# A Performer attention and MLP-Mixer kernel on one core: batch 1's keys loaded ahead of the first half of w_ch1, with an order of the work found anew

## The chip, the core and the metric

The kernel runs on one core of one Trainium2 chip. The core has TensorE (PE, with its weight loads PEld), VectorE (DVE), ScalarE (ACT), GpSimd (POOL) and SyncE (SP), and DMA engines that all of them feed. The metric is the device time in microseconds of one execution; the median over seven runs before the change is 288.76.

## What is computed

Eight batches, eight heads, 576 positions, head size 64, 128 random features; then a mixer of 512 channels with 256 token features and 1536 channel features.

```python
def phi(x):
    proj = np.einsum('bhsd,md->bhsm', x, omega)
    sq = np.sum(x * x, axis=-1, keepdims=True) / 2.0
    h = proj - sq
    h = h - np.max(h, axis=-1, keepdims=True)
    return np.exp(h) / np.sqrt(m)
q_p, k_p = (phi(q_s), phi(k_s))          # q_s, k_s: q and k times 1/sqrt(sqrt(D))
kv = np.einsum('bhsm,bhsd->bhmd', k_p, v)
z = np.sum(k_p, axis=2)
num = np.einsum('bhsm,bhmd->bhsd', q_p, kv)
den = np.einsum('bhsm,bhm->bhs', q_p, z)[..., None] + 1e-06
x = num / den                             # heads side by side: (8, 576, 512)
...
h = np.maximum(xt @ w_tok1, 0.0) @ w_tok2 # xt: x with positions and channels swapped
u = x + h.transpose(0, 2, 1)
h2 = np.maximum(u @ w_ch1, 0.0) @ w_ch2
return u + h2
```

## The kernel before

**Stages.** For each batch `attention` makes the features of keys (L638) and queries (L652) as matmuls with the transposed omega, takes exponentials on ACT (L514), the maximum over the features of each key and its reciprocal on DVE (L664, L666), scales v by it on POOL (L671, tile `vs`), sums keys times v on PE (L684, then a copy, L701), and forms numerator and denominator on PE (L720, L722), which DVE divides (L729, L730) or, for two heads of batch 0, ACT (L742). The last 64 positions of every head (the "tail") are packed together: L546 and L558 or L514 (`kpt`) for keys, L611 (`qpt`) for queries, and the tile `vbd`, which POOL makes (L562, L565, L596), holds their v. `token_mix` (batch 0: `token_mix_first`, L803 to L825) follows with w_tok1 and w_tok2; `channel_mix` multiplies by w_ch1 (L854; for the first two blocks of batch 0 L860 and L862), applies the relu (L874, L876), multiplies by w_ch2 (L892) and stores through SP. `token_tail` (L835) does the token mixing of two batches' tails together. From batch 1 on the attention of a batch is interleaved on PE with the channel mixing of the batch before.

**Loads.** Keys of batch 0 are loaded in four pieces from ACT's and SP's queues (`load_first`, L397). Everything else that is cast to 16 bits goes through POOL's queue: q, v and tails of batch 0 (L313, L331, L324, L345), w_tok1 (L432, L436), w_tok2 (L438), the halves of w_ch1 (`load_wc1`, L444), batch 1's keys (`load_nat(1, "k", 0, 8, ...)`, again L313), their tail and v's tail, the second half of w_ch1, batch 1's queries and v, and the two halves of w_ch2 (L459). Queries and keys of batches 0 and 1 are transposed on PE (L485, tails L505). Those of later batches are cast into DRAM (L353, L358, L364) and come back transposed through SP (L374).

**What sets the order.** Every piece of work is a `Job` with an engine, a planned cost, a key and dependencies. `Planner.run` walks through a planned time: of the jobs of an engine that can start first, the one with the lowest key is taken, and it calls the function that issues the instructions. So each engine's instruction order is fixed when the program is built. A DMA job has also a planned length `wire`; all planned transfers run one after the other, a transfer's data is taken to be there `AFTER` behind its end, and PE is planned to start `MARGIN` (or a smaller value for a transfer) behind what it needs. `LANES` is 8: a queue's DMA is planned to wait for the one eight before it. A DMA on POOL comes after the one that stands before it in the code (`job.after`), whatever the keys say. The keys are tables of numbers: `HEAD` for batch 0 and the loads of the head, `NEAR` for batches 1 and 2, `KEYS` for the rest. Until the first channel mixing, the planner fills planned idle time of PE with matmuls of zeros into free banks (L943), which keep PE busy and compute nothing of the result.

Of the kernel before, what the change touches and what calls it, by code (L numbers as in the profile page):

```python
# [13 lines left out]
AX = mybir.AxisListType  # L14


KEYS = {"a": -1.349, "as": 0.099, "t": -1.509, "ts": 0.187, "gv": 2.165, "lt": -2.428, "lv": -3.989, "to": -2.341, "tt": 0.635, "ks": 1.094, "km": 0.303, "vs": -0.113, "l1": -0.452, "kt": -0.062}
NEAR = {"1": {"a": -1.734, "as": 0.259, "t": -2.775, "ts": 0.45, "gv": -0.056, "km": -2.03, "vs": -0.397, "kt": 0.253}, "2": {"a": -2.686, "as": 0.0, "t": -0.603, "ts": 0.324, "gv": -1.313, "km": 3.931, "vs": 0.571, "lv": -3.347, "lt": -2.872, "kt": -0.122}}
HEAD = {"kp": [-3.838, -3.822, -3.881, -3.404], "ke": [-2.728, -2.927, -2.827, -2.727], "km": [-4.039, -3.592, -4.221, -2.25], "vs": [-3.448, -3.487, -3.196, -2.472], "qp": [-3.203, -3.403, -3.303, -3.488], "qe": [-3.328, -3.374, -2.153, -3.748], "kv": [-3.407, -3.257, -2.676, -3.133], "ko": [-2.32, -3.035, -3.463, -3.168], "n": [-3.199, -3.47, -3.182, -2.377, -2.999, -3.268, -2.999, -2.899], "no": [-4.124, -3.487, -3.919, -3.144, -3.226, -3.426, -3.126, -2.386], "ktm": -3.643, "kt": -4.584, "kte": -5.022, "qt": -3.759, "qte": -5.587, "kx": [-6.213, -5.658, -5.326, -5.458], "kxo": [-6.855, -7.05, -5.723, -4.783], "ktx": -5.661, "ktxo": -5.912, "qx": [-4.987, -3.488], "qxo": [-4.073, -2.977], "qtx": -4.584, "qtxo": -3.371, "t1": [0.229, -1.008, -0.737, -0.359], "re": [0.072, -0.781, 0.181, -0.024], "ut": [0.056, -0.48, -0.104, -0.341], "uo": [-0.099, -0.259, -0.108, 0.38], "vbd": -8.41, "w1": -9.7, "w1t": -9.38, "w2t": -9.78, "wa": -8.03, "wb": -9.17, "w2": -10.08}
BY = {"kx": "ADDD", "ktx": "A", "qx": "DD", "qtx": "A", "ko": "DADD", "re": "AAAA", "uo": "AADD", "no": "DDADDADD", "r0": "AAAAADAAADAA", "ko1": "DDAA", "r1": "AAAAAAAAAAAA"}  # L20


# [15 lines left out]
class Planner:  # L38
# [5 lines left out]
    MARGIN = {"PE": 0.3, "ACT": 0.05, "DVE": 0.05, "POOL": 0.05, "SP": 0.0}  # L44
    LANES = 8
    BEFORE = {"POOL": 1.5, "SP": 0.8, "ACT": 0.8}
    AFTER = 0.8
    SWITCH = 0.1
    COLD = 5.5

# [25 lines left out]
    def run(self):  # L76
# [6 lines left out]
        while any(waiting.values()):  # L83
            choice = None
            for eng, jobs in waiting.items():
                ready = []
                for j in jobs:
                    t = at[eng]
                    ok = True
                    if j.after is not None and j.after.end is None:  # L90
                        continue
                    for d in j.deps:
                        if d.end is None:
                            ok = False
                            break
                        m = self.MARGIN[eng] if d.eng != eng else (-self.LATENCY["PE"] if eng == "PE" else 0.0)
                        if eng == "PE" and self.warm is not None:
                            m = min(m, 0.05)
                        if eng == "PE" and d.wire:
                            m = 0.5  # L100
                        t = max(t, d.end + m)
                    if not ok:
                        continue
                    self.now = t
                    got = []
                    for tag, name in j.take:
                        if (tag, name) in self.held:
                            continue
                        one = self.find(tag, got)
                        if one is None:  # L110
                            ok = False
                            break
                        got.append((tag, one[0]))
                        t = max(t, one[1])
                    if not ok:
                        continue
                    if j.wire and len(lanes[eng]) >= self.LANES:
                        t = max(t, lanes[eng][-self.LANES])
                    key = j.key - (KEYS["ks"] if eng == "PE" and j.rows and last_rows == j.rows else 0.0)
                    ready.append((t, key, j))  # L120
                if not ready:
                    continue
                first = min(r[0] for r in ready)
                t, _, j = min((r for r in ready if r[0] <= first + 1e-6), key=lambda r: r[1])
                if choice is None or t < choice[0]:
                    choice = (t, j)
# [3 lines left out]
            t, j = choice  # L130
            eng = j.eng
            waiting[eng].remove(j)
            if self.warm is not None and eng == "PE":
                if j.heavy:
                    self.warm = None
                else:
# [9 lines left out]
                    t = max(t, at["PE"])  # L146
# [31 lines left out]
def kernel(  # L178
# [12 lines left out]
    nc = tc.nc  # L191
# [129 lines left out]
    def load_nat_tail(b, w, key, deps=()):  # L321
        o = 0 if w == "q" else ST
        def go():
            nc.gpsimd.dma_start(  # L324
                out=nat["t", b][o : o + ST].rearrange("p i e -> p (i e)"), in_=src[w][b, :, SM:S, :].rearrange("h (g f) d -> h g (f d)", g=8)
            )
        ld[w + "t", b] = dma("POOL", key, 0.4, go, deps, cost=0.6)

    def load_v(b, key, deps=(), h0=0, h1=H):
        def main():  # L330
# [5 lines left out]
    def load_v_tail(b, key, deps=()):  # L336
        jobs = []
        for g in range(2):
            def tails(g=g):
                if b < NPE:  # L340
                    o, i = t_vt[place("vt", b)][:, g, :], v[b, 4 * g : 4 * g + 4, SM:S, :].rearrange("h (r e) d -> h r (e d)", e=2)
                else:
                    o = t_vt[place("vt", b)][g * ST : (g + 1) * ST].rearrange("p a (c d) -> p (a c) d", c=2)
                    i = v[b, :, SM:S, :].rearrange("(a i) t d -> i t a d", i=2)[g]
                nc.gpsimd.dma_start(out=o, in_=i)  # L345
            jobs.append(dma("POOL", key + 0.01 * g, 0.22 if b < NPE else 0.4, tails, take=[("vt", b)], deps=deps, cost=0.7))
        ld["vt", b] = jobs[-1]

    def load_transposed(b, key, deps=()):
# [45 lines left out]
    def load_first(h0, h1, eng, key):  # L395
        def go():
            (nc.sync if eng == "SP" else nc.scalar).dma_start(  # L397
                out=first_k[:, h0:h1, :], in_=k[0, h0:h1, 0:SM, :].rearrange("h (p j) d -> p h (j d)", j=NJ))
        job = dma(eng, key, 0.37 * (h1 - h0), go, cost=0.47)
        for h in range(h0, h1):  # L400
            ld["k", 0, h] = job

# [32 lines left out]
    def load_w1t(o, key):  # L435
        j_w1t.append(dma("POOL", key, 0.2, cost=0.58, fn=lambda: nc.gpsimd.dma_start(out=w1t[o * ST : (o + 1) * ST, o, :], in_=moe_w_tok1[SM:S, :]), deps=[j_w1tz]))  # L436
    load_w1t(0, HEAD["w1t"])
    j_w2 = dma("POOL", HEAD["w2"], 1.7, lambda: nc.gpsimd.dma_start(out=w2, in_=moe_w_tok2.rearrange("(i p) s -> p i s", p=P)))  # L438
    def w2_of(tb, j):
        return w2[:, tb, 0:SM].rearrange("p (c j) -> p j c", j=NJ)[:, j, :]  # L440
    j_wc1 = []
    def load_wc1(i):
        c0 = i * (DC // 2)
        j_wc1.append(dma("POOL", HEAD[("wa", "wb")[i]], (3.9, 4.4)[i], lambda: nc.gpsimd.dma_start(  # L444
            out=wc1[:, :, c0 : c0 + DC // 2], in_=moe_w_ch1[:, c0 : c0 + DC // 2].rearrange("(i p) c -> p i c", p=P))))
    load_wc1(0)
    load_nat(1, "k", 0, 8, -9.61)
    load_nat_tail(1, "k", -3.48)
    load_v_tail(1, -3.46)
    load_wc1(1)  # L450
# [525 lines left out]
```

The softmax here doesn't subtract the row's maximum and nothing guards it: scores larger than these inputs give would overflow.

## Time and profile before

| | us |
|---|---|
| median of 7 runs | 288.76 |
| lowest, highest | 288.64, 289.54 |
| profiled execution | 288.68 |
| its span in the profile | 286.8 |
| batch 0's channel mixing starts (first L860) | 26.43 |
| batch 0's product with w_ch2 starts (first L892) | 43.90 |
| first and last PE instruction | 1.20, 282.7 |

The profile is of one execution; times in it count from the start of its span. A line of the order of time gives start, length, engine, source line, operation, what is written and read, and in brackets the idle time of the engine before it with what ended it. Runs of equal instructions are merged, so a length is that of the whole run, with the pipeline's end in it: eight matmuls of 512 columns show 1.9 us, while the next one starts 1.73 us after the first. Landings of single DMAs are read from the trace's semaphore events.

### The profile page before, as it was taken

How to read it: one execution, taken by the hardware profiler on the slowest of the kernel's cores; microseconds unless marked ns; L12 is line 12 of the kernel's file. 1: busy time of each engine (PE TensorE's matmuls, PEld its weight loads, DVE VectorE, ACT ScalarE, POOL GpSimd, SP SyncE). 2: the span in 40 equal slices, each digit the busy share in tenths (PEclk: the TensorE clock that was granted, in tenths of full speed). 3: DMA queues.
4: the chain of work that ended last, by engine and by line, in shares of the span. 5: the costliest groups of instructions: out<-in, count | busy, mean ns of one | idle time of the engine just before them, and what ended most of it. 6: DMA issues, size and time to landing. Idle time of an engine off the chain costs nothing.

```text
span 286.8 us, 5605 instructions
## 1 busy us (share of the span) xinstructions
PE 279.7 (98%) x2186; PEld 140.7 (49%) x2186; DVE 152.3 (53%) x330; ACT 153.8 (54%) x322; POOL 93.8 (33%) x126
## 2 busy tenths in 40 slices
PE   7999999999999999999999999999999999999994
PEld 3576454445544544455445544554455444444442
DVE  4886854546669624845584647564686231031012
ACT  3995872098449552875386528753576402602600
POOL 8995940157015701480148016601141000000000
PEclk9999999999999999999999999999999999999999
DMA  8999999999966995999799988996621042013013
GB/s 191 191 201 194 202 213 152 210 228 155 166 97 161 140 173 114 214 152 185 111 197 157 201 112 146 199 199 82 129 74 39 0 110 112 0 49 115 2 45 101
DMA packets 85721, 39.59 MB, mean 138 GB/s; under 512 B 64384, under 2 KB 80128, under 8 KB 85504
## 3 DMA queue, kind: packets, MB, share of 16 engines
q0 software_dynamic: 34288, 17.45, 44.1%
q1 hardware_dynamic: 50624, 21.01, 33.5%
q10 hardware_dynamic: 784, 0.79, 0.8%
q8 instruction: 17, 0.28, 0.4%
q14 instruction: 8, 0.07, 0.1%
HBM read 35.88 MB, written 16.52 MB: 183 GB/s over the span
## 4 chain that ended last, share of the span: by engine, by line
PE 94%; ACT 2%; DMA 2%; issue 0%; SPq 0%; DVE 0%; DVEq 0%; ACTq 0%
PE bank L892 33%; PE bank L854 32%; PE bank L776 4%; PE bank L759 4%; PE bank L684 3%; PE bank L720 3%; PE bank L652 3%; PE bank L638 3%; DMA wc<-in_k_dram 2%; PE bank L760 1%; ACT kp L514 1%; PE bank L485 1%; PE bank L835 1%; PE bank L722 1%; PE bank L803 1%; PE bank L819 1%
## 5 line engine op out<-in xcount | busy, mean ns | idle before, releaser
L892 PE MATMUL bank<-wc,r 128*128 128x512 f16 (+2 forms) x444 | 100.7, 374 | 0.0
L874 ACT ACTIVATE r<-bank 128x512 f16<-128x512 f32 x106 | 62.7, 606 | 64.5 <-PE bank L854 64.4
L854 PE MATMUL bank<-uT,wc 128*128 128x512 f16 x376 | 88.7, 379 | 0.0
L892 PEld LDWEIGHTS <-r 128*128 128x128 f16 x444 | 40.9, 98 | 48.9 <-issue 4.4
L854 PEld LDWEIGHTS <-wc 128*128 128x128 f16 x424 | 39.7, 98 | 43.0 <-issue 0.4
L514 ACT ACTIVATE qp<-bank 128x512 f16<-128x512 f32 x64 | 35.6, 640 | 13.0 <-PE bank L652 13.0
L664 DVE TENSOR_REDUCE km<-kp 128x8 f16<-128x1024 f16 x32 | 38.5, 1202 | 2.3 <-ACT kp L514 2.3
L514 ACT ACTIVATE kp<-bank 128x512 f16<-128x512 f32 x64 | 34.6, 626 | 6.6 <-PE bank L638 6.4
L901 DVE TENSOR_TENSOR o<-u,bank 128x512 f32<-128x512 f16 x28 | 19.1, 683 | 34.5 <-PE bank L892 34.5
L671 POOL TENSOR_TENSOR vs<-v,vs 128x512 f16<-128x512 f16 x32 | 33.3, 1063 | 12.5 <-PE bank L722 3.6
L730 DVE TENSOR_TENSOR x<-bank,rc 128x320 f16<-128x320 f32 x62 | 30.5, 492 | 2.1
L779 DVE TENSOR_TENSOR u<-x,bank 128x512 f16<-128x512 f16 x28 | 17.4, 682 | 9.5 <-PE bank L776 9.5
L729 DVE RECIPROCAL rc<-bank 128x5 f32<-128x5 f32 x62 | 11.5, 186 | 16.0 <-PE bank L722 15.7
L596 POOL TENSOR_TENSOR vbd<-vt,vbd 128x512 f16<-128x512 f16 (+1 forms) x7 | 8.2, 1176 | 32.7 <-PE bank L835 14.5
L380 POOL COPY junk<-kT 128x1 f16<-128x1 f16 x6 | 1.1, 188 | 52.3 <-DMA kT<-k 52.3
L767 DVE TENSOR_SCALAR r<-bank 128x512 f16<-128x512 f32 x7 | 4.8, 692 | 21.1 <-PE bank L760 21.1
L759 PE MATMUL bank<-x,w1m 128*128 128x512 f16 x56 | 14.4, 379 | 0.0
L720 PEld LDWEIGHTS <-qp 128*128 128x128 f16 x256 | 12.3, 98 | 4.0
L684 PEld LDWEIGHTS <-kp 128*128 128x128 f16 x256 | 11.1, 98 | 5.7 <-issue 1.1
L684 PE MATMUL bank<-vs,kp 128*128 128x65 f16 x256 | 12.9, 193 | 0.7 <-ACT r L874 0.7
L720 PE MATMUL bank<-kvsb,qp 128*128 128x65 f16 x256 | 13.5, 193 | 0.0
L776 PE MATMUL bank<-r,w 128*128 128x512 f16 x56 | 13.4, 380 | 0.0
(109 smaller groups left out, 267.6 us busy)
## 6 DMA issues: line engine op xcount, KB each, us to landing
out_dram<-o SPq DMA_DIRECT2D x32, 256.0 KB, 2.5
q<-in_q_dram POOLq DMA_DIRECT2D x6, 576.0 KB, 7.0
wc<-in_moe_w_ch_dram POOLq DMA_DIRECT2D x4, 768.0 KB, 10.7
k<-in_k_dram POOLq DMA_DIRECT2D x6, 512.0 KB, 8.7
v<-in_v_dram POOLq DMA_DIRECT2D x6, 512.0 KB, 7.4
r<-in_q_dram POOLq DMA_DIRECT2D x4, 256.0 KB, 7.6
v<-in_v_dram POOLq DMA_DIRECT2D x4, 256.0 KB, 7.5
out_dram<-o SPq DMA_DIRECT2D x5, 128.0 KB, 2.3
```

Of the source, the lines that this page charges most:

```text
L514: nc.scalar.activation(out=out, in_=in_, func=AF.Exp, bias=0.0, scale=1.0)
L664: nc.vector.reduce_max(out=mx, in_=kpv, axis=AX.X)
L671: nc.gpsimd.tensor_tensor(out=vs[:, :, 0:D], in0=t_v[place("v", b)][:, hh[0] : hh[0] + 2, :].rearrange("p h (j d) -> p (h j) d", d=D), in1 ...
L684: nc.tensor.matmul(ps[:, i, :], kpv[:, 2 * i + j // 2, j % 2, :], vs[:, i * NJ + j, 0 : D + 1], start=(i == 0 and j == 0), stop=False, ski ...
L720: nc.tensor.matmul(ps[:, k, j * 65 : (j + 1) * 65], st, s[:, i, 0 : D + 1], start=True, stop=True)
L730: nc.vector.tensor_tensor(out=t_x[place("x", b)][:, :, (2 * hp + hs[0]) * D : (2 * hp + hs[0] + n) * D].rearrange("p j (i d) -> p i j d", ...
L759: nc.tensor.matmul(ps, w1m[:, j, tb * P : (tb + 1) * P], x[:, j, :], start=(j == 0), stop=False)
L776: nc.tensor.matmul(ps, w2_of(tb, j), r1[:, tb, :], start=(tb == 0), stop=(tb == NT - 1))
L854: nc.tensor.matmul(ps, wc1[:, db, cb * P : (cb + 1) * P], moving(db), start=(db == 0), stop=(db == ND - 1))
L874: nc.scalar.activation(out=o, in_=bank(n), func=AF.Relu)
L892: nc.tensor.matmul(ps[:, cols], r3[:, cb, j * P : (j + 1) * P], wc2[:, cb, cols], start=(cb == 0), stop=(cb == NCB - 1))
L901: nc.vector.tensor_tensor(out=t_o[place("o", (c, j))][:, cols], in0=uu[:, cols], in1=bank(n)[:, cols], op=ALU.add)
```

## The change

Three things change in the text. The load of batch 1's keys is written ahead of the first half of w_ch1, and gets a key of its own. The planned lengths of loads and the planner's `AFTER` and margin for transfers get other values. All three tables of keys get other numbers, and with them the order of the instructions on every engine changes, in the head and in the later batches; `BY`, which says which engine does a copy, stays.

```diff
-KEYS = {"a": -1.349, "as": 0.099, "t": -1.509, "ts": 0.187, "gv": 2.165, ...
+KEYS = {"a": -1.308, "as": 0.122, "t": -1.391, "ts": 0.239, "gv": 0.565, ...
-NEAR = {"1": {"a": -1.734, "as": 0.259, "t": -2.775, ...
+NEAR = {"1": {"a": -1.622, "as": 0.295, "t": -3.984, ...
-HEAD = {"kp": [-3.838, -3.822, -3.881, -3.404], "ke": [-2.728, -2.927, -2.827, -2.727], ...
+HEAD = {"wk": -9.02, "kp": [-3.734, -3.822, -3.934, -3.404], "ke": [-3.2, -2.984, -2.827, -2.702], ...
...
-    AFTER = 0.8
+    AFTER = 1.15
...
                         if eng == "PE" and d.wire:
-                            m = 0.5
+                            m = 0.2
...
-        ld[w + "t", b] = dma("POOL", key, 0.4, go, deps, cost=0.6)
+        ld[w + "t", b] = dma("POOL", key, 0.5 if b else 0.4, go, deps, cost=0.6)
...
-            jobs.append(dma("POOL", key + 0.01 * g, 0.22 if b < NPE else 0.4, tails, ...
+            jobs.append(dma("POOL", key + 0.01 * g, 0.4 if b else 0.22, tails, ...
...
-        job = dma(eng, key, 0.37 * (h1 - h0), go, cost=0.47)
+        job = dma(eng, key, (0.5 if h0 == 6 else 0.37) * (h1 - h0), go, cost=0.47)
...
-    j_w2 = dma("POOL", HEAD["w2"], 1.7, ...
+    j_w2 = dma("POOL", HEAD["w2"], 2.1, ...
...
-        j_wc1.append(dma("POOL", HEAD[("wa", "wb")[i]], (3.9, 4.4)[i], ...
+        j_wc1.append(dma("POOL", HEAD[("wa", "wb")[i]], (3.9, 3.7)[i], ...
+    load_nat(1, "k", 0, 8, HEAD["wk"])
     load_wc1(0)
-    load_nat(1, "k", 0, 8, -9.61)
     load_nat_tail(1, "k", -3.48)
     load_v_tail(1, -3.46)
     load_wc1(1)
```

What the built programs show of it in the head, in POOL's order from w_tok1 on (times stand for nothing here, only the order):

```
before: w_tok1, its tail, w_tok2, vbd, vs 0, w_ch1 a, keys 1, vs 1 and 2, key tail 1, vs 3, v tail 1, w_ch1 b, ...
after:  w_tok1, vbd, its tail, w_tok2, vs 1, vs 0, vs 2, keys 1, w_ch1 a, key tail 1, vs 3, v tail 1, w_ch1 b, ...
```

On ACT the four exponentials of the key tail (L558) stand before the last key exponential in the old order, and behind the copy of q's tail, both `qpt` and the first two `qp` exponentials in the new one. On DVE the maxima of head pairs 0, 1 and 2 come before the copies of q and before the maximum that L558 needs (L552). On PE half of batch 1's key transposes (L485) come ahead of their tail's (L505), and of the matmuls L652 of batch 1 the first four come ahead of the first L684 instead of behind it. There are 26 fillers instead of 23.

## The prediction

> **What bounds the kernel now.** I read the page's shares and its chain first, then busy time by stretch, then the order of time on PE, POOL and ACT over the first 45 us.
>
> ```profile
> span 286.8 us, 5605 instructions
> PE 279.7 (98%) x2186; PEld 140.7 (49%) x2186; DVE 152.3 (53%) x330; ACT 153.8 (54%) x322; POOL 93.8 (33%) x126
> ...
> PE 94%; ACT 2%; DMA 2%; issue 0%; SPq 0%; DVE 0%; DVEq 0%; ACTq 0%
> ```
>
> TensorE is the bound. The stretches (length, then busy us of PE, PEld, DVE, ACT, POOL, clock, DMA share, GB/s) say where anything can still be won or lost:
>
> ```profile
> 0.00:26.42 26.42, 24.16 (x294) 15.55 (x294) 18.05 (x54) 17.47 (x46) 23.93 (x36) 1.00 1.16 195
> 26.42:43.90 17.48, 16.78 (x178) 9.23 (x175) 13.44 (x31) 14.04 (x30) 10.88 (x12) 1.00 1.31 200
> 43.90:282.80 238.90, 238.80 (x1724) 115.97 (x1720) 120.57 (x245) 122.29 (x248) 59.04 (x78) 1.00 0.72 128
> 282.80:286.80 4.00, 0.00 (x0) 0.00 (x0) 0.29 (x1) 0.00 (x0) 0.00 (x0) 1.00 0.29 84
> ```
>
> After 43.90 PE is full (238.80 of 238.90) and the last 4.0 us are a store. So the change is decided by when L892, batch 0's last product, starts, and by what the new order costs after it. PE's own order of time:
>
> ```profile
> 23.46 0.29 PE L505 MATMUL bank<-ident,r 64*128 64x64 f16 x4
> 26.43 1.47 PE L860 MATMUL bank<-uT,wc 128*128 128x512 f16 x6
> 33.79 1.90 PE L854 MATMUL bank<-uT,wc 128*128 128x512 f16 x8
> 36.38 0.40 PE L684 MATMUL bank<-vs,kp 128*128 128x65 f16 x8 [0.69 <-ACT r L874]
> 43.90 2.54 PE L892 MATMUL bank<-wc,r 128*128 128x512 f16 x11
> ```
>
> Eight L854 issue in 1.73 us (0.216 each), so the work from 33.79 is issued by 35.52 and PE stands until 36.38: 0.86 us. The profile names ACT, but POOL's first batch-1 scaling (35.25 plus 1.05) also ended only at 36.30.
>
> ```profile
> 12.30 0.81 POOL L444 DMA_DIRECT2D wc<-in_moe_w_ch_dram  x1
> 13.10 0.89 POOL L313 DMA_DIRECT2D r<-in_k_dram  x1
> 14.01 2.08 POOL L671 TENSOR_TENSOR vs<-v,vs 128x512 f16<-128x512 f16 x2
> 23.08 0.75 POOL L331 DMA_DIRECT2D v<-in_v_dram  x1 [1.25 <-DMA r<-in_k_dram]
> 28.22 0.83 POOL L459 DMA_DIRECT2D wc<-in_moe_w_ch_dram  x1 [2.08 <-PE bank L638]
> 35.25 4.10 POOL L671 TENSOR_TENSOR vs<-v,vs 128x512 f16<-128x512 f16 x4
> ```
>
> The loads form one line: landings follow issue order, and at 195 to 200 GB/s it is full to about 42 us. Landings in the trace: w_tok2 16.32, first half of w_ch1 20.09, batch 1's keys 22.79 (2.70 later), their tail 23.42, second half of w_ch1 27.70, last half of w_ch2 41.83. POOL's load at 23.08 waited for the load eight before it (landed 22.79), and the one at 28.22 stands eight behind the 27.70 landing: at most eight are out.
>
> **The change, part by part.** No computation is removed. The planner's constants (DMA lengths, margins, keys) issue nothing themselves; their cost is the order that comes out, and I take that from the changed program's instruction lists. Matmuls are the same but for 26 fillers (L943) instead of 23: 3 x 0.22 us, on the path only where real work was ready. The keys' DMA and the first w_ch1 half swap; both issues (0.89 and 0.81 us) stay, nothing on SP moves in the head. But on POOL three scalings (L671, 1.05 us each) instead of one now stand ahead of both issues, and the vbd work (2.17 us) ahead of w1t and w_tok2, whose line is full until 14.7 and hides that.
>
> *Loads.* The third scaling reads the second half of v, landed at 13.47: it runs 13.55 to 14.6, and the keys issue at 14.6 instead of 12.30 for the first of the pair. How soon can an idle line start? POOL's v load issued at 194.50 shows it:
>
> ```profile
> 194.00:195.00 1.00, 1.00 (x6) 0.49 (x5) 0.00 (x0) 0.56 (x1) 0.62 (x2) 1.00 0.00 0
> 195.00:196.00 1.00, 1.00 (x7) 0.42 (x5) 0.48 (x1) 0.04 (x1) 0.47 (x1) 1.00 0.00 0
> 196.00:197.00 1.00, 1.00 (x6) 0.47 (x5) 0.21 (x1) 0.60 (x1) 0.00 (x0) 1.00 0.57 58
> ```
>
> No packet until 196.20, 1.70 us after the issue. So the keys' packets start at 16.3; before, the next load's packets took over at about 15.4 (w_tok2's run out between 15.0 and 16.0). The line idles 0.9 us (bounds: 0, if other packets cover it, and 1.7), and every later load lands 0.9 late: keys 19.3 (3.5 earlier), w_ch1 half 23.7 at most against its first use after 26, tail 24.3, second w_ch1 half 28.6.
>
> The Trainium skill, "DMA: Bandwidth & Descriptors", section "Anatomy of one DMA — SWDGE (gpsimd) path", fits a POOL-issued DMA as 2.0 us plus bytes over 436 GB/s: 3.2 us for 512 KB. By it the keys would land at 17.8, nothing behind them would be late, and the total would fall by 0.2; the trace's line moves 195 GB/s, and I keep that.
>
> *ACT in the head.* These are its lines now:
>
> ```profile
> 10.84 1.19 ACT L558 ACTIVATE kpt<-bank,kt_nb 128x128 f16<-128x128 f32 x4
> 12.31 1.17 ACT L514 ACTIVATE qp<-bank 128x512 f16<-128x512 f32 x2
> 17.38 1.14 ACT L742 ACTIVATE x<-bank,rc 128x64 f16<-128x64 f32 x5
> ```
>
> ACT is busy from 8.17 to 17.38 because the kpt exponentials (1.0) fill the wait for q. In the new order they stand behind qT, qpt and two qp, which wait for q's tail (landed 12.14), and the DVE makes their bias after three maxima. Step by step: the first kp group moves ahead of the third transpose, 5.54 not 5.98 (0.44 gained), so kp exponentials end 9.55 for three pairs; the fourth needs a DVE copy that follows the first maximum (8.50 plus 0.65) and a PE slot behind q's transposes (landed 8.84): 10.4 to 11.45. Idle to 12.5 (q tail), its copy to 13.0, idle to 13.5, qpt to 14.1, two qp to 15.1, kpt to 16.1, then five qp and a small copy to 19.1. So L742 starts at 19.1, 1.7 late, and L684 of head pair 0 at 16.1. Its consequence: three L684 groups at once (1.1), L720 at 17.25, DVE's two scalings 0.58 each, and the first L803 at 18.8 instead of 17.29.
>
> *PE from there.* Until L860: four L803 groups 0.56 each, numerators 0.6, filler 0.22, four L819/L821 groups 0.86 each, transposes 0.22 + 0.46 + 0.55, L546 0.22, L638 0.55, two changes of row mode 0.11 each: 8.7. L860 starts at 27.5, against 26.43 (there 9.14, with 0.3 of waits and one L684 group, now done earlier): +1.1. The key tail at 24.3 is wanted at 24.9, so it hides; if ACT were on time it would be the next thing late.
>
> *To L892.* L652 (0.54) now stands ahead of the L684 that waited. From 27.5 the row sums (L860 1.40, L638 0.55, L505, L862 and modes 0.75, three L854 x8 of 1.73, two L485 about 0.5, L611 0.3, L652 0.55) give 37.4. POOL: its issue at 28.22 becomes 29.1, then 0.85 + 1.9 (vbd) + 0.55 + 1.7 + 0.6 + 1.3 = 36.0 and the first scaling ends 37.1, 0.8 late, just covered. If ACT's delay were absent, POOL would set 37.1 instead: the gain is capped. From there four L684 groups (0.36 each), sixteen L854 (0.216 each), four numerator pairs (0.30 each) and the other L652 with their changes of mode (0.85) take 6.95; the scalings end every 1.05 us from 37.1 and stay ahead of their L684 groups. L892 starts at 44.3, +0.4. Bounds: +0.15 (POOL alone) and +1.1 (nothing recovered).
>
> *After L892.* Each change between half-row matmuls (L546, L611, L638, L652, L835) and full ones costs 0.11 us; there are 52 instead of 54: -0.2. In batch 2 all four L638 groups now stand together; the last needs a bank that ACT's exponential frees about 0.6 later, given back in part: +0.1. Stalls before were 0.8 in all there; the new order could save those or add one like the 0.86 above: bounds -0.8 and +0.9.
>
> **Sum.** +0.4 - 0.2 + 0.1 = +0.3 on the span of 286.8: 287.1. The profiled execution took 288.68, 0.08 under the median 288.76, so 289.0.
>
> **Rivals.** *Slower, by ACT's gap in the head:* its place is 9.5 to 16.1 on ACT, its price the 1.1 us at L860, and it decides if L892 starts after 44.6. For it: ACT executes in order, and q's landing does not move. Against: the L652 ahead of the waiting L684 should return 0.6. With all of 1.1 kept, 289.7.
> *Faster, by the filled stall:* if the loads do not idle and ACT keeps pace, L652 fills 0.55 of the 0.86, and one more wait of 0.2 goes: 288.68 - 0.75 = 287.9. For it: the keys land long before use. Against: the v landing at 13.47 holds POOL, whatever ACT does.
> *The earlier keys are hidden anyway and the head ends even:* only the mode changes count, 288.5.
>
> **How the numbers follow.** Forecast 0.40, slower rival 0.38, faster 0.10, even 0.12. This kernel can tell about 0.2% (0.58 us) from nothing: slower means above 289.34, faster below 288.18. Forecast and even case lie within: same 0.50; slower 0.40; faster 0.10. The range takes the forecast, the even case and the slower rival with some of the stall bound: 288.3 to 290.0.
>
> **What would show it.** Right: keys landed near 19.3 and their tail near 24.3; ACT's first L742 near 19.1; L860 near 27.5; L892 near 44.3; PE full after it. Wrong: ACT without gaps between 9.5 and 13.5, the DMA share unbroken at 15 to 16.5, a PE stall after 44, or L892 before 43.7.

## The result and the profile after

The changed kernel takes 290.27 us (median of 25 runs, 289.49 to 291.42); the kernel before takes 289.13 (median of 60 runs, taken beside them). The ratio is 1.0035, 95% interval 1.0026 to 1.0043: about 1.0 us slower. The forecast was 289.0, no change that can be told, with the range ending at 290.0. It started from the 288.76 of seven runs; the kernel before stands 0.37 higher in the sixty runs here, so that part of the way to 290.27 is the base and not the change. The profiled execution took 289.70, its span is 287.8.

The page of the changed kernel, the lines that answer to those shown of before:

```profile
span 287.8 us, 5607 instructions
PE 281.1 (98%) x2189; PEld 141.8 (49%) x2189; DVE 152.5 (53%) x330; ACT 152.8 (53%) x322; POOL 93.3 (32%) x126
...
PE 88%; POOL 5%; DMA 3%; ACT 2%; issue 1%; DVE 0%; POOLq 0%; ACTq 0%; DVEq 0%
```

PE still has 98%, but its part of the chain that ended last fell from 94% to 88%; POOL now has 5% and transfers 3% (2% before). Busy time by stretch, cut at the same events as before (first L860, first L892, the last store):

```profile
0.00:28.31 28.31, 25.65 (x297) 16.69 (x298) 17.95 (x53) 17.67 (x46) 23.88 (x36) 1.00 1.13 185
28.31:45.03 16.72, 16.72 (x178) 9.01 (x175) 13.75 (x31) 14.02 (x30) 10.88 (x13) 1.00 1.31 202
45.03:283.80 238.77, 238.64 (x1724) 116.14 (x1720) 120.40 (x245) 121.11 (x248) 58.57 (x78) 1.00 0.75 128
283.80:287.80 4.00, 0.13 (x3) 0.00 (x0) 0.40 (x2) 0.00 (x0) 0.00 (x0) 1.00 0.34 100
```

The stretch up to L860 grew from 26.42 to 28.31 (+1.89), the one from L860 to L892 shrank from 17.48 to 16.72 (-0.76), the rest from 238.90 to 238.77 (-0.13). So the loss lies in the first 28 us. PE is idle there for 2.66 us (28.31 less 25.65) against 2.26 before (26.42 less 24.16); the rest of the 1.89 counts as busy, and part of that is the three more fillers, which compute nothing of the result. PE's order of time names the longest wait that is new:

```profile
25.79 0.29 PE L505 MATMUL bank<-ident,r 64*128 64x64 f16 x4 [0.83 <-DMA r<-in_k_dram]
...
28.31 1.47 PE L860 MATMUL bank<-uT,wc 128*128 128x512 f16 x6
...
35.69 1.90 PE L854 MATMUL bank<-uT,wc 128*128 128x512 f16 x8
37.52 0.61 PE L652 MATMUL bank<-qT,omT 64*128 64x512 f16 x4
38.06 0.42 PE L684 MATMUL bank<-vs,kp 128*128 128x65 f16 x8
...
45.03 1.67 PE L892 MATMUL bank<-wc,r 128*128 128x512 f16 x7
```

L652 stands ahead of L684 and the old stall of 0.86 is gone. In its place PE waits 0.83 at L505, the transpose of batch 1's key tail, for that tail's load. POOL's queue shows why the load is late (in this kernel POOL, SP and ACT issue the DMAs; PE and DVE issue none):

```profile
11.14 3.09 POOL L671 TENSOR_TENSOR vs<-v,vs 128x512 f16<-128x512 f16 x3
14.17 0.95 POOL L313 DMA_DIRECT2D r<-in_k_dram  x1
15.12 0.76 POOL L444 DMA_DIRECT2D wc<-in_moe_w_ch_dram  x1
15.86 0.60 POOL L324 DMA_DIRECT2D r<-in_k_dram  x1
...
24.39 0.75 POOL L331 DMA_DIRECT2D v<-in_v_dram  x1 [2.76 <-DMA wc<-in_moe_w_ch_dram]
...
29.77 0.82 POOL L459 DMA_DIRECT2D wc<-in_moe_w_ch_dram  x1 [1.44 <-issue]
...
36.56 4.10 POOL L671 TENSOR_TENSOR vs<-v,vs 128x512 f16<-128x512 f16 x4
```

The keys are issued at 14.17 behind three scalings. Landings in the trace: w_tok2 16.70 (before 16.32), keys 20.21 (22.79), first half of w_ch1 24.10 (20.09), key tail 25.75 (23.42), second half of w_ch1 29.25 (27.70). So the keys are 2.58 earlier, and the tail, which L505 needs, is 2.33 later. It lands 1.65 behind the load ahead of it, w_ch1's first half; before, it landed 0.63 behind the load ahead of it, the keys.

### The profile page after: what moved, and what is told of

It is laid out like the page before. It is cut to its first block, busy times and chain, and to the rows that moved or that the text cites. A ratio compares the mean times of both kernels' runs of the same rounds, so it can differ in the third digit from the quotient of the medians.

```text
span 287.8 us, 5607 instructions
## 1 busy us (share of the span) xinstructions
PE 281.1 (98%) x2189; PEld 141.8 (49%) x2189; DVE 152.5 (53%) x330; ACT 152.8 (53%) x322; POOL 93.3 (32%) x126
## 3 DMA queue, kind: packets, MB, share of 16 engines
q0 software_dynamic: 34288, 17.45, 44.6%
## 4 chain that ended last, share of the span: by engine, by line
PE 88%; POOL 5%; DMA 3%; ACT 2%; issue 1%; DVE 0%; POOLq 0%; ACTq 0%; DVEq 0%
PE bank L892 32%; PE bank L854 32%; PE bank L776 4%; PE bank L759 4%; DMA r<-in_k_dram 3%; PE bank L684 3%; PE bank L720 2%; PE bank L638 2%; PE bank L652 2%; ACT qp L514 1%; PE bank L760 1%; POOL vs L671 1%; POOL r L313 1%; PE bank L835 1%; POOL vbd L565 1%
## 5 line engine op out<-in xcount | busy, mean ns | idle before, releaser
L892 PE MATMUL bank<-wc,r 128*128 128x512 f16 (+2 forms) x444 | 99.9, 374 | 0.0
L874 ACT ACTIVATE r<-bank 128x512 f16<-128x512 f32 x106 | 63.4, 613 | 54.2 <-PE bank L854 53.5
L854 PE MATMUL bank<-uT,wc 128*128 128x512 f16 x376 | 88.3, 379 | 0.1
L892 PEld LDWEIGHTS <-r 128*128 128x128 f16 x444 | 41.2, 98 | 49.9 <-issue 4.4
L854 PEld LDWEIGHTS <-wc 128*128 128x128 f16 x424 | 39.7, 98 | 42.7 <-issue 0.5
L514 ACT ACTIVATE kp<-bank 128x512 f16<-128x512 f32 x64 | 35.2, 618 | 23.3 <-PE bank L638 23.3
L901 DVE TENSOR_TENSOR o<-u,bank 128x512 f32<-128x512 f16 x28 | 19.1, 682 | 33.7 <-PE bank L892 33.6
L720 PEld LDWEIGHTS <-qp 128*128 128x128 f16 x256 | 12.2, 98 | 4.3 <-issue 0.2
L720 PE MATMUL bank<-kvsb,qp 128*128 128x65 f16 x256 | 13.3, 193 | 0.0
L684 PE MATMUL bank<-vs,kp 128*128 128x65 f16 x256 | 12.8, 193 | 0.3 <-POOL vs L671 0.3
L684 PEld LDWEIGHTS <-kp 128*128 128x128 f16 x256 | 10.7, 98 | 4.1 <-issue 0.5
```

Source lines behind the costliest of these rows:

```text
L514: nc.scalar.activation(out=out, in_=in_, func=AF.Exp, bias=0.0, scale=1.0)
L684: nc.tensor.matmul(ps[:, i, :], kpv[:, 2 * i + j // 2, j % 2, :], vs[:, i * NJ + j, 0 : D + 1], start=(i == 0 and j == 0), stop=False, ski ...
L720: nc.tensor.matmul(ps[:, k, j * 65 : (j + 1) * 65], st, s[:, i, 0 : D + 1], start=True, stop=True)
L854: nc.tensor.matmul(ps, wc1[:, db, cb * P : (cb + 1) * P], moving(db), start=(db == 0), stop=(db == ND - 1))
L874: nc.scalar.activation(out=o, in_=bank(n), func=AF.Relu)
L892: nc.tensor.matmul(ps[:, cols], r3[:, cb, j * P : (j + 1) * P], wc2[:, cb, cols], start=(cb == 0), stop=(cb == NCB - 1))
```

## The experiments

Theory 1: three scalings ahead of the keys' issue leave the line of loads idle, and what is late behind it is the loss. Theory 2: the head's new order on the engines is the loss. In each kernel the planner makes its order from the file's own tables, single jobs are moved in it, and then everything is issued; with no moves the instructions come out in exactly the file's order.

```python
def issue(self, moves):
    seq = self.sequence
    for eng, n, before in moves:
        of = [i for i, s in enumerate(seq) if s[0] == eng]
        a, b = of[n], of[before]
        job = seq.pop(a)
        seq.insert(b if b < a else b - 1, job)
    for _, fn, _ in seq:
        fn()
```

An entry moves an engine's job number `n` ahead of its job number `before`. Where that is said, the planner is run a second time with the moved order given, and chooses PSUM banks and fillers anew; PE's numbers leave the fillers out then. What the profiles show of all runs, in us (tail: landing of batch 1's key tail; POOL: start of its first batch-1 scaling; ratios of runs in one set go against the same runs of the kernel before):

| kernel | tail | wait at L505 | L860 | POOL | L892 | ratio to before (95%) |
|---|---|---|---|---|---|---|
| before | 23.42 | 0 | 26.43 | 35.25 | 43.90 | 1 |
| changed | 25.75 | 0.83 | 28.31 | 36.56 | 45.03 | 1.0035 (1.0026 to 1.0043) |
| changed, again | 26.42 | 1.03 | 28.98 | 37.34 | 45.70 | 1.0019 (0.9999 to 1.0039) |
| keys early | 23.25 | 0 | 27.58 | 35.40 | 44.30 | 1.0003 (0.9985 to 1.0021) |
| keys ahead of one scaling | 25.04 | 0 | 27.64 | 36.58 | 44.66 | 1.0009 (0.9997 to 1.0022) |
| tail ahead | 21.02 | 0 | 27.58 | 36.92 | 45.00 | 1.0034 (1.0021 to 1.0046) |
| tail ahead, vbd ahead | 21.34 | 0 | 28.01 | 36.82 | 44.90 | 1.0024 (1.0005 to 1.0042) |
| before, swap only | 23.70 | 0.41 | 26.71 | 35.39 | 44.05 | 1.0007 (0.9992 to 1.0022) |
| before, three scalings first | 26.86 | 2.21 | 31.30 | 38.47 | 47.73 | 1.0124 (1.0106 to 1.0142) |
| before, L652 ahead | 23.79 | 0.18 | 26.80 | 35.42 | 43.86 | 0.9995 (0.9984 to 1.0006) |
| before, L652 and scalings ahead (part of batch 1 scaled wrongly) | 24.05 | 0.31 | 27.06 | 34.39 | 46.76 | 1.0156 (1.0132 to 1.0180) |
| old head, new body | 23.48 | 0.10 | 26.49 | 35.14 | 43.22 | 0.9974 (0.9956 to 0.9992) |
| the same, again | 23.90 | 0.49 | 26.91 | 35.38 | 43.63 | 0.9980 (0.9964 to 0.9996) |
| keys early, q early | 23.24 | 0 | 27.45 | 35.10 | 44.17 | 0.9980 (0.9971 to 0.9989) |
| keys early, L720 ahead | 23.37 | 0 | 27.79 | 35.64 | 44.51 | 1.0001 (0.9986 to 1.0016) |
| both (q early, L720 ahead) | 23.18 | 0 | 27.53 | 35.17 | 44.25 | 0.9977 (0.9968 to 0.9986) |

**Keys early.** The keys and w_ch1's first half are issued ahead of the three scalings.

```diff
 MOVES = [
+    ("POOL", 16, 13),
+    ("POOL", 17, 14),
 ]
```

> The changed kernel, with only POOL's issues of batch 1's keys and of w_ch1's first half moved ahead of its three scalings. Theory 1 (the loads' line stood idle behind the three scalings and the key tail came 2.33 us later than before, which cost PE 0.83 at L505): the keys' first packets follow w_tok2's without a gap, the tail lands near 23.3, L505 waits for nothing, L860 starts near 27.5 instead of 28.31, L892 near 44.2 instead of 45.03, and the run takes 0.8 us less than the changed kernel, 289.4 where that takes 290.3 and the kernel before 289.1. Theory 2 (ACT's new order in the head sets the end: the batch-1 exponentials behind q's work, L803 1.4 later): L505 no longer waits, but L860 and L892 stay within 0.2 of the changed kernel's, and so does the time.

L505 waits for nothing, and L892 starts 0.73 earlier than in the changed kernel:

```profile
25.06 0.29 PE L505 MATMUL bank<-ident,r 64*128 64x64 f16 x4
27.58 1.47 PE L860 MATMUL bank<-uT,wc 128*128 128x512 f16 x6
44.30 2.54 PE L892 MATMUL bank<-wc,r 128*128 128x512 f16 x11
```

The median, 289.20, is that of the kernel before in the same set, 289.15; the ratios' intervals of this kernel and of the changed one don't overlap. The line in the changed kernel between 15 and 18 us (the last two columns are the DMA share and GB/s):

```profile
15.00:16.00 1.00, 0.87 (x15) 0.59 (x14) 0.34 (x2) 1.00 (x5) 1.00 (x3) 1.00 0.28 13
16.00:17.00 1.00, 1.00 (x28) 0.84 (x25) 0.30 (x1) 1.00 (x3) 0.98 (x2) 1.00 0.90 59
17.00:18.00 1.00, 0.73 (x22) 0.70 (x20) 0.94 (x4) 1.00 (x4) 1.00 (x2) 1.00 1.23 165
```

And with the keys early:

```profile
15.00:16.00 1.00, 0.87 (x11) 0.43 (x10) 0.21 (x1) 1.00 (x5) 1.00 (x2) 1.00 1.33 181
16.00:17.00 1.00, 1.00 (x28) 0.88 (x25) 0.30 (x1) 1.00 (x4) 0.99 (x2) 1.00 1.47 198
17.00:18.00 1.00, 0.84 (x22) 0.77 (x20) 0.77 (x3) 1.00 (x4) 1.00 (x2) 1.00 1.43 203
```

Over these three us the changed kernel moves 13 + 59 + 165 = 237 KB, the other 582: at 195 GB/s that is 1.8 us of line time lost. For this part of the loss theory 1 holds; theory 2's part stays out of the difference, since PE, ACT and DVE have the same order in both.

**Tail ahead.** Only the key tail is issued earlier, ahead of w_ch1's first half.

```diff
 MOVES = [
+    ("POOL", 18, 17),
 ]
```

> The changed kernel, with only the issue of the key tail moved ahead of that of w_ch1's first half; the three scalings stay ahead of the loads and the line stays idle. Theory 1 in its narrow form (of the late loads only the tail matters): the tail lands near 21.5, w_ch1's halves near 24.7 and 29.3, L505 waits for nothing, and the time falls by the same 0.8 us as with the early keys. If it falls by clearly less while L505's wait is gone, another late load (w_ch1's first half at L819 and L860, or its second) takes the wait over, and the idle line matters as a whole. Theory 2: the wait goes, the time stays.

L505's wait goes, L860 starts at 27.58 as with the keys early, and the time stays that of the changed kernel (290.21). The narrow form of theory 1 is false: the 0.73 won at L860 is lost again before L892. PE's order there:

```profile
36.95 0.60 PE L652 MATMUL bank<-qT,omT 64*128 64x512 f16 x4
38.05 0.40 PE L684 MATMUL bank<-vs,kp 128*128 128x65 f16 x8 [0.50 <-POOL vs L671]
```

The rest of the idle line arrives here over POOL. Its last w_ch2 issue waits for the load eight before it, the second half of w_ch1. In five profiles that half lands at 27.70, 27.86, 29.25, 29.28 and 29.62 (before, keys early, changed, keys ahead of one scaling, tail ahead), and the issue starts at 28.22, 28.38, 29.77, 29.80 and 30.14, always 0.52 later. Behind it in POOL's order stand `vbd`, the casts and the scalings that L684 needs.

**The same with vbd ahead of that issue.**

```diff
 MOVES = [
     ("POOL", 18, 17),
+    ("POOL", 31, 30),
 ]
```

> The changed kernel with the key tail ahead of w_ch1's first half (as in the run that took L505's wait away and kept the time), and one more move on POOL: the last w_ch2 issue behind the batch-1 vbd product instead of ahead of it. Theory 1, second path (POOL's in-order queue stands at that issue until the load eight before it, w_ch1's second half, has landed, and so its batch-1 scalings come late): POOL no longer stands there, its first batch-1 scaling starts near 36.2 instead of 36.92, the 0.50 wait of L684 goes, L892 starts near 44.4 instead of 45.00, and the time falls by about 0.6 to 289.6. Rival: POOL waits for DVE's vbd at 29.9 anyway, or something else takes the wait over; the scalings and the time stay.

L684 waits no more, and L860 to L892 takes 16.89 instead of 17.42. But the scaling starts at 36.82, only 0.10 earlier than with the tail ahead alone, and L892 at 44.90 (expected 36.2 and 44.4). The rival came true in part: POOL's `vbd` product starts at 29.88, just behind DVE's part of it (L587, ended 29.79) and the landing of w_ch1's second half (29.81). And this execution's head ran 0.43 later, so PE came that much later to L684, which takes most of the wait away by itself. The median fell by 0.3, to 289.89, in another set, and the ratios' intervals overlap. What the move is worth isn't told; that POOL is late for L684 behind the late load rests on the trace of the tail ahead.

**Keys ahead of one scaling.** A dose between the two: the keys' issue moves to 13.31, w_ch1's stays behind the third scaling.

```diff
 MOVES = [
+    ("POOL", 16, 15),
 ]
```

> The changed kernel with the keys' issue ahead of the third scaling only, so two of the three stay ahead of it; w_ch1's first half and the tail are issued after the third. Theory 1 with the price read from the traces (1.75 us from issue to first packet): the issue moves from 14.17 to about 13.2, the first packet to 14.9, before w_tok2's packets run out near 15.5, so the line never idles: keys near 18.9, w_ch1's half near 22.8, the tail near 23.4, L505 waits for nothing, and the time is that of the early keys (289.2, 0.9 us below the changed kernel). If it is the number of scalings, and not the idle line, about a third of that is gained.

Half came true. L505 waits for nothing, but the line does not stay full: 73, 158 and 200 GB/s in the same three us, and 164 and 148 in the two after them, since w_ch1's half is now issued at 15.28. Over these five us it moves 743 KB, the early keys 1006 and the changed kernel 639: about 1.3 us of line time lost, against 1.9. Keys land at 19.42, but w_ch1's halves at 24.39 and 29.28, no earlier than in the changed kernel (24.10 and 29.25), and POOL's first batch-1 scaling starts as there (36.58 and 36.56). What differs is the tail: it lands at 25.04, 0.65 behind w_ch1's half instead of 1.65, just in time. L892 is 0.36 later than with the keys early and 0.37 earlier than in the changed kernel. So, as far as single profiles tell, about half of the 0.73 comes over POOL from the late half of w_ch1, and the other half from the tail. The ratio, 1.0009, can't be told from that of the early keys.

**The swap alone, in the kernel before.**

```diff
 MOVES = [
+    ("POOL", 15, 14),
 ]
```

> The kernel before, with the one move that the change is named for: the keys' issue ahead of that of w_ch1's first half, POOL's scalings and everything else in the order of before. Expected: keys land near 19, w_ch1's half near 22.8, the tail still near 23.4, PE's order is the same and so is its start of L860 (26.43) and L892 (43.90): no more than 0.2 us from the kernel before. If instead the swap itself costs, w_ch1's half lands after 26.4 or PE's start of L860 moves.

Keys land at 19.15, w_ch1's half at 23.01, the tail at 23.70; L892 moves by 0.15, the time by less than can be told. L505 waits 0.41 and L860 moves by 0.28, but with the loads in the old order it waits too in some profiles (0.18 with L652 ahead, 0.49 in the old head's second one). The move that the change is named for costs and gains nothing by itself that these runs can tell.

**Three scalings first, in the kernel before.**

```diff
 MOVES = [
+    ("POOL", 16, 14),
+    ("POOL", 17, 15),
 ]
```

> The kernel before, with one thing taken from the change: all three of POOL's first scalings (L671) stand ahead of the issue of w_ch1's first half and of the keys, instead of one. ACT, DVE and PE keep their order. Theory 1 (an idle line is what costs): the two issues move from 12.3 and 13.1 to about 15.0 and 15.8, the line idles, w_ch1's half lands near 21.5, the keys near 24.2, their tail near 24.9 (before 23.42); L505, wanted at 23.46, waits some 1.3 us, L860 starts near 27.7, POOL's first batch-1 scaling near 36.4, and the run takes 0.6 to 1.2 us more than the kernel before. Theory 2 (ACT's order in the head is what costs): within 0.2 us of the kernel before.

The direction is right and the size is three to six times too small: 292.76, 3.9 us more. POOL's second and third scaling had to wait for DVE first, because DVE makes their reciprocals later in this order:

```profile
13.78 2.07 POOL L671 TENSOR_TENSOR vs<-v,vs 128x512 f16<-128x512 f16 x2 [1.57 <-DVE vs L666]
15.79 0.81 POOL L444 DMA_DIRECT2D wc<-in_moe_w_ch_dram  x1
```

So the line was idle until 17, the tail landed 3.44 later than before, and PE stood from about 24.7 to 26.91. That brought a second loss, told in the last section; and at 19.22 an L684 of batch 0 had waited 1.12 for POOL's fourth scaling, which now stands behind three late issues. The run shows that late loads, with the order of before on ACT, DVE and PE, make the kernel slower; it doesn't size the changed kernel's loss.

**L652 ahead, in the kernel before.** The part of the change that fills the stall of 0.86, alone.

```diff
 MOVES = [
+    ("PE", 85, 84),
+    ("PE", 86, 85),
 ]
```

> The kernel before, with batch 1's first two L652 products put ahead of the first L684 of batch 1, which waited 0.86 us for POOL and ACT: the part of the change that fills this stall, alone. If the stall is time on the path, the time falls by 0.4 to 0.8 us (two L652 groups of row-mode products issue in it). The rival: the L652 products bring two more changes of row mode (0.11 each) and the wait only moves to the next L684, which POOL still sets; then less than 0.2 us.

The rival won: L892 at 43.86. PE's order:

```profile
35.80 0.61 PE L652 MATMUL bank<-qT,omT 64*128 64x512 f16 x4
36.55 0.40 PE L684 MATMUL bank<-vs,kp 128*128 128x65 f16 x8
...
38.56 0.40 PE L684 MATMUL bank<-vs,kp 128*128 128x65 f16 x8 [0.28 <-POOL vs L671]
```

The stall is filled, and the third L684 then waits for POOL, whose scalings come every 1.05 us.

**L652 and POOL's scalings ahead, in the kernel before.** The four scalings also go ahead of batch 2's v tails.

```diff
 MOVES = [
     ("PE", 85, 84),
     ("PE", 86, 85),
+    ("POOL", 37, 35),
+    ("POOL", 38, 36),
+    ("POOL", 39, 37),
+    ("POOL", 40, 38),
 ]
```

> The kernel before with batch 1's first two L652 products ahead of the first L684 of batch 1 (which alone moved L892 by 0.04 and the time by less than could be told), and POOL's four batch-1 scalings ahead of the two small v loads (L345) of batch 2 that precede them. If POOL's scalings pace the three L684 of batch 1, as the 0.28 wait for POOL in the run with L652 alone says: they start near 34.1 instead of 35.4, L684 waits for nothing, L892 starts near 43.1, and the time is 0.5 to 0.8 us below the kernel before. If the row-mode changes and the other waits eat what L652 fills, the time stays within 0.2 us of the kernel before.

293.88 us, and no answer. In this kernel the last scaling is also issued ahead of the reciprocal that it should use, so part of batch 1 is scaled by batch 0's values; DVE's reciprocal then waits 4.49 us for POOL, and PE 3.19 for DVE. The question went to the next kernel.

**Old head, new body.** The changed kernel with the head in the order of before: the first 41 jobs of PE, 34 of ACT, 33 of DVE and 20 of POOL (planner run a second time).

```diff
+HEADS = {
+    'PE': [0, 1, 2, 4, 3, 6, 7, 5, 8, 11, 10, 9, 15, 16, 12, 13, 19, 14, ...
+    'ACT': [0, 1, 2, 3, 4, 7, 5, 6, 8, 9, 10, 17, 18, 11, 15, 16, 12, 19, ...
+    'DVE': [0, 1, 2, 3, 4, 5, 6, 7, 8, 10, 9, 15, 13, 12, 11, 14, 17, 16, ...
+    'POOL': [0, 1, 2, 3, 4, 5, 6, 7, 8, 9, 11, 12, 10, 14, 17, 16, 13, 15, 18, 19],
+}
...
+    for eng, head in HEADS.items():
+        of = self.plan[eng]
+        of[: len(head)] = [of[n] for n in head]
```

> The changed kernel from the first batch-1 products on (L546 on PE), with the whole head (PE's first 41 jobs, ACT's 34, DVE's 33 and POOL's 20) in the order of the kernel before: the body of the change alone. The prediction's term for the body (L652 fills the stall of 0.86, then two fewer row-mode changes): L860 starts near 26.5 as before, L892 at 43.1 to 43.9, and the time is 0 to 0.8 us below the kernel before. How much depends on POOL, whose first batch-1 scaling still ends near 36.3: theory 1 with POOL as the next bound says that L684 waits for it and no more than 0.2 us is left of the 0.86.

> The best version so far, the changed kernel's body behind the head of before, again, to narrow its time (288.28 against 288.88 in the first set). The terms: L892 starts 0.68 earlier than before and the body after it takes 0.13 less, so 0.5 to 0.9 us below the kernel before. In the first profile two L684 waited 1.6 us for POOL near 156 us, behind a late load; if this is the order's doing it is there again, and the gain is smaller than the terms say.

L860 at 26.49, L892 at 43.22, and no wait for POOL:

```profile
35.70 0.61 PE L652 MATMUL bank<-qT,omT 64*128 64x512 f16 x4
36.27 0.40 PE L684 MATMUL bank<-vs,kp 128*128 128x65 f16 x8
...
37.48 0.41 PE L684 MATMUL bank<-vs,kp 128*128 128x65 f16 x8
```

The new body puts eight L854 and numerators between the L684 groups, so POOL's 1.05 us steps are covered. The gain of 0.68 is the body's (0.27 in the second profile, where L505 waits 0.49 for the tail); the cap that theory 1 put on it did not hold. Two sets give 0.9974 (0.9956 to 0.9992) and 0.9980 (0.9964 to 0.9996): 0.6 us faster than the kernel before. The wait of 1.6 us for POOL near 156 us in the first profile (execution 289.66) is missing in the second (288.18), so the order does not bring it every time. The executions spread more than those of the other kernels, from 287.49 to 289.87 and one of 293.0.

**The changed kernel again.**

> The changed kernel once more, unchanged, for a second profile. If the line's idle and slow start behind POOL's three scalings are the order's doing, this execution shows them too: under 80 GB/s between 15 and 17 us, keys near 20.2, key tail between 24.7 and 25.8, a wait of L505 between 0 and 0.9. If the tail again lands 1.65 behind w_ch1's half (0.5 to 0.6 in the other orders), that delay belongs to the order as well; if it lands 0.6 behind, it was that one execution's.

The idle line is there again (40, 21 and 106 GB/s from 15 to 18), L505 waits 1.03, and the tail lands 1.91 behind w_ch1's half. The v that the third scaling reads landed at 13.51 here and at 12.69 in the first profile, and the keys' issue stands at 14.64 instead of 14.17: that is 0.47 of the 0.67 by which the tail is later than in the first profile. The tail's own delay, 1.65 and 1.91 behind the load ahead of it where all other orders show 0.45 to 0.74, came in both executions of this order. It hangs on little: with the keys ahead of one scaling the tail lands 0.65 behind, and the small load after it (L345) another 0.86. Its cause stays open. A 16 KB packet of the instruction queue is under way from 23.69 to 24.63 in the first profile, but the kernel before has one too, from 22.58 to 23.54, and its tail lands on time at 23.42. The ratio of this set, 1.0019 (0.9999 to 1.0039), is less sure than that of the first.

**What the head's order costs.** The early keys and the old head differ in the head's order (and in the planner's second run; the kernel with L720 ahead, below, has that run too and gains nothing): L860 27.58 against 26.49, L892 44.30 against 43.22, or 43.63 in the old head's second profile. That is the place of the 1.1 us that the prediction laid on ACT. Three kernels, all with the early keys and a second planner run, ask for its cause. The first moves q's copy on DVE, the first L652 and their exponentials ahead:

```diff
 MOVES = [
     ("POOL", 16, 13),
     ("POOL", 17, 14),
+    ("DVE", 13, 11),
+    ("DVE", 15, 13),
+    ("PE", 15, 12),
+    ("PE", 16, 13),
+    ("ACT", 15, 12),
+    ("ACT", 16, 13),
+    ("ACT", 17, 15),
+    ("ACT", 18, 16),
 ]
```

> The changed kernel with the keys and w_ch1's first half issued early (which gave back 0.9 us) and, in the head, DVE's copy of q's first half ahead of its second and third maximum, the batch-0 maximum of kt ahead of the third, and the first two L652 products and their exponentials on ACT ahead of q's tail. Theory 2 for the remaining 1.08 us at L892 between the early keys (44.30) and the head of before (43.22): ACT idles 0.99 and 0.59 us for q because DVE copies q late; with the copy early ACT idles under 0.5 us there, L742 starts near 17.8, L803 near 17.9, L860 near 26.7, L892 near 43.5, and the time is 0.3 to 0.9 us below the early keys. Rival: PE's L684 wait for POOL's scalings instead (ends at 15.9 and 17.6), and the gain stays under 0.3.

With the early keys alone ACT had stood for q, as predicted:

```profile
12.33 0.37 ACT L509 COPY qT<-bank 128x256 f16<-128x256 f16 x1 [0.99 <-PE bank L505]
13.29 0.76 ACT L514 ACTIVATE qpt<-bank 128x256 f16<-128x256 f32 x2 [0.59 <-PE bank L611]
```

Now it doesn't, and stands at L742 instead:

```profile
11.47 1.09 ACT L514 ACTIVATE qp<-bank 128x512 f16<-128x512 f32 x2
...
18.73 1.13 ACT L742 ACTIVATE x<-bank,rc 128x64 f16<-128x64 f32 x5 [0.59 <-DVE rc L739]
```

L803 moves from 18.85 to 18.52 only, L892 by 0.13. The second kernel puts two L720 groups, which L739 and L742 need, ahead of the fourth L684, with ACT as in the changed kernel; the third does both.

```diff
+    ("PE", 25, 24),
+    ("PE", 26, 25),
```

> The changed kernel with the early keys, and on PE the two L720 groups that L742 waits for ahead of the fourth L684 of batch 0 (which needs POOL's fourth scaling, done at 17.6) instead of behind it, as in the kernel before; ACT and DVE as in the changed kernel. If ACT's idle time alone makes the head late (the prediction's reading), L742 still starts near 18.9 and L803 near 18.8, L892 within 0.2 of 44.30. If that L684 alone does, L742 starts near 17.5, L803 near 17.7, L860 near 26.5, L892 near 43.3, and the time falls by 0.9 us against the early keys. If both hold it in parallel: little is gained here.

> Both moves: q's copy, its first L652 and their exponentials early (ACT's idle time gone; alone this moved L803 from 18.85 to 18.52), and the two L720 groups ahead of the fourth L684. If ACT and that L684 hold L803 in parallel, L742 now starts near 17.4, L803 near 17.5, L860 near 26.5, L892 near 43.2 to 43.5, and the time is 0.6 to 1.0 us below the kernel before (288.2 to 288.6). If a third thing holds it (DVE's maxima, POOL's scalings for the first three L684, which end at 15.9), L803 stays above 18.2 and L892 above 43.9.

L803 at 19.07 and 18.81: neither moves it. In the third ACT and PE both wait for DVE's L739 (0.36 and 0.39), whose work starts only once the first three L684 are through, at 15.76 to 16.7; in the kernel before the first L684 stood at 12.65. None of the three kernels brought L892 near 43.5, as it was expected if their move were the cause. The kernels with q early are 0.6 us faster than the kernel before in their medians (0.9980, 0.9977), more than the traces' 0.1 earlier L892 explains; the interval of the early keys is too wide to settle that. Which single move makes the head late stays open; that the old head with the same body starts L860 earlier is shown, by 1.1 and 0.7 us in two profiles.

## Why the prediction was wrong, point by point

Three kernels take the change apart at L892: 43.90 before; 43.22 with the new body (-0.68); 44.30 with the new head's order too (+1.08); 45.03 with the loads behind the scalings (+0.73). The sum is the measured +1.13, against +0.4 predicted. Single executions differ by up to 0.7 in these places (see the repeats), as much as one step; but the ratios, 0.9974, 1.0003 and 1.0035, go the same way. In time the change added 1.0 us where 0.3 was forecast; the rest of the way to 290.27 is the higher base.

*What bounds the kernel.* Right: after L892 PE is full, and the loss is decided before it.

*Loads: the step that failed.* The issue at 14.6 was right (14.17 and 14.64), and so was the first packet 1.70 later (15.83 and 16.30, 1.66 behind the issue). "The line idles 0.9 us", and with it every later load 0.9 late, was too small: the line lost 1.8 us, because it starts again slowly, 59 GB/s and 165 in the first two us. The prediction's own row of the POOL load at 194.50 had 58 GB/s in the us of its first packets, and the next us of that profile has 145; only the delay was read from it. In the second execution, with the issue where it was predicted, the keys came at 20.68, not 19.3, w_ch1's halves at 24.51 and 30.02, not 23.7 and 28.6. The Trainium skill's fit ("DMA: Bandwidth & Descriptors", section "Anatomy of one DMA — SWDGE (gpsimd) path"), by which the keys would land 3.2 us behind their issue, is further off: it took 6.04 here. The fit is per DMA, with nothing of what the line does before it; here the line's 195 to 200 GB/s and its slow start decided.

*"The key tail at 24.3 is wanted at 24.9, so it hides": false.* The tail came at 25.75. L505 waited 0.83, and L860 came at 28.31 instead of 27.5. Two things are in this: the line's slow start, and a delay of the tail's own, 1.65 behind w_ch1's half instead of some 0.6, that no term of the sum had. With the usual 0.6 it would have landed near 24.7 and hidden, since PE was ready for it at 24.96; so the wait hangs on the tail's own delay, whose cause is open. The loss does not hang on it alone. The prediction's second cover, POOL's first scaling "ends 37.1, 0.8 late, just covered", was thin too: w_ch1's second half came at 29.25 instead of 28.6, and the scaling ended at 37.6. With the tail ahead PE waits 0.50 for it, and with the keys ahead of one scaling, where the tail is in time, L892 is still 0.36 late. The upper bound of 1.7 on the idle line, set in the paragraph on loads, would have put the tail at 25.1, past 24.9; it was kept for the range and not carried through to L505 and POOL.

*ACT in the head.* The numbers were right (L742 18.77, predicted 19.1; L803 18.69, predicted 18.8; L860 27.58 without the late loads, predicted 27.5), and the gaps on ACT too. The cause was told too simply: without ACT's gaps for q L803 comes 0.33 earlier, not 1.5. That the numbers fit is then partly luck.

*To L892.* L652 in the stall, and POOL next in line: right. From L860 to L892 it took 16.72, predicted 16.8. The rows listed for the way to L684 add up to 9.24, so to 36.7 and not to the 37.4 given; it took 9.75 (28.31 to 38.06), so 9.9 was near, but not by the rows listed. POOL's issue came at 29.77 instead of 29.1, for the late loads again; under L505's wait it cost nothing, and without that wait 0.50.

*After L892.* Predicted -0.1, measured -0.13.

*The rivals.* The slower one was priced for ACT's gap in the head kept whole, at 289.7. Its sign was right, and its 1.1 at L860 is there (27.58 against 26.49); but the body gave 0.68 of it back, and its condition, L892 after 44.6, came true through the loads. The faster one, with the stall filled, no idle line and ACT on time, is the old head with the new body: 0.6 us faster in time, priced at 0.8. The swap itself is hidden, as the even case says.

## What to carry to other kernels

A load's issue that moves behind work on its queue cost more here than its own delay, because the line of loads ran dry: count the delay to the first packet and the slow start, and carry the upper bound through to every consumer, not only into the range. When one wait is taken away, look for the next consumer of the same late resource: here the tail's wait on PE hid POOL's wait for the load eight before. An order found anew mixes gains and losses; taken apart into head and body, the body's half is worth 0.6 us (0.9974 and 0.9980) without the other.

## What the runs showed of the hardware

PE's clock fell in one wait and stayed full in a longer one. With three scalings first, PE stood from about 24.7 to 26.91 and the granted clock (the column ahead of the DMA share) went to half:

```profile
26.00:27.00 1.00, 0.10 (x2) 0.10 (x3) 0.00 (x0) 0.00 (x0) 0.30 (x1) 0.84 1.19 209
27.00:28.00 1.00, 1.00 (x12) 0.91 (x12) 0.43 (x1) 0.00 (x0) 1.00 (x2) 0.50 1.13 206
28.00:29.00 1.00, 1.00 (x8) 1.00 (x6) 0.69 (x1) 0.00 (x0) 1.00 (x3) 0.50 1.20 218
29.00:30.00 1.00, 1.00 (x7) 0.16 (x5) 0.00 (x0) 0.00 (x0) 0.75 (x1) 0.50 1.20 186
30.00:31.00 1.00, 1.00 (x22) 0.73 (x22) 0.77 (x2) 0.66 (x2) 0.00 (x0) 0.95 1.43 197
```

Eight L485 took 1.04 us there instead of 0.61, and L505 to L860 4.39 instead of 2.97: 1.4 us on top of the wait. The waits of 0.83 and 1.03 in the changed kernel left the clock at 1.00, and so did the longest of all, in the kernel before with L652 and the scalings ahead:

```profile
38.00:39.00 1.00, 0.00 (x0) 0.00 (x0) 0.49 (x2) 0.00 (x0) 1.00 (x2) 1.00 1.26 211
39.32 0.61 PE L652 MATMUL bank<-qT,omT 64*128 64x512 f16 x4 [3.19 <-DVE qT L492]
```

The Trainium skill, "TensorE: Matmul & The Clock Gate", Part 1, has the clock halved after an idle window of about 3.4 us, and back after as long a busy one. The way back about agrees (3.4 us at half, by the rows from 26 to 31, PE busy for the last 3.2 of them). On the way down a rest of 2.2 us was enough in one execution, and 3.19 us was not in another: the length of the rest alone doesn't decide in these runs.

The line's slow start behind an idle stretch was seen in each of three profiles: 59 and 165 GB/s in the changed kernel, 21 and 106 in its second execution, 37 and 117 with three scalings first (17 to 19 us), against 195 to 210 when it is full. Why it starts slowly wasn't tried.
